# An adaLN transformer block on one core: the first pairs' modulation split over two PSUM banks by engine, and w1's load gated by the b2 row

## The chip, the core and the metric

The kernel runs on one core of a Trainium2 chip. A core has TensorE (PE, matmuls; PEld is its weight loads), VectorE (DVE), ScalarE (ACT), GpSimd (POOL) and SyncE (SP, which issues most of the DMAs). Each engine works its own instruction list in order and waits for others through semaphores. The metric is the device time of one execution in microseconds. In a row of the order below, a name with `<-` is what an instruction writes and reads.

## What is computed

One transformer block on x of 2048 tokens by 448 features, with 16 heads of 28 and a hidden size of 1792:

```python
mod = (_silu(c) @ w_mod).reshape(c.shape[0], 6, 1, -1)      # sa, ca, ga, sb, cb, gb
h = _layernorm(x) * (1 + ca) + sa
x = x + ga * attention(h, A_wqkv, A_wo)    # each query sees 8 keys, 2 tokens apart, behind it
h = _layernorm(x) * (1 + cb) + sb
x = x + gb * (gelu(_layernorm(h) @ w1 + b1) @ w2 + b2)
```

## The kernel before

The tokens are split into 1024 rows by two halves s (even and odd tokens), so that a window with stride 2 becomes a dense window of 8 rows within a half. Eight "pairs" j of 128 rows hold both halves. Features are cut into 14 blocks of 64, two to a partition range, so a pair's transposed activations hT have 7 blocks kb of 128 partitions (the lower 64 hold one half's features, the upper the other's).

The function `build_plan` lists 669 operations with the tiles that they read and write. It also holds cost estimates for a planner that ran beforehand; they issue nothing. The planner's result is written in the file: the table ORDER names each operation and its engine (96A is operation 96 on ScalarE, D is VectorE, P TensorE, G GpSimd, S SyncE, X a DMA's landing), and SLOTS gives the buffer of each tile. The kernel issues the operations in that order, so each engine's instruction list follows from ORDER alone. A layer under it adds the semaphore waits. It lets no two engines work on one PSUM tile at a time, not even where both only read.

The front, up to about 21 us, goes like this:

- SyncE loads x, the modulation weights (w_mod) and the raw query and key weights. The raw weights land in a staging tile, which shares its memory with w1 and is printed as `w`.
- "wpad" operations (L249 on ScalarE, L251 on VectorE and GpSimd) copy these weights into a padded layout, 28 columns into 32. There are 20 of them: for each kb, the part with m=0 serves the first half of the projection and the part with m=4 the second. They wait for three landings of the staging tile.
- VectorE and ScalarE take the layer norm's statistics (L365 to L370) and normalise the first two pairs (L386, L390) into zb.
- TensorE computes the modulation columns (L338, L341), which VectorE turns into the per-partition constants sa_c and ca_c (L352, L353). Then it transposes the two pairs' zb blocks (L430) into two PSUM tiles: blocks 0 to 3 into one and 4 to 6 into the other.
- The "hmod" operations (L401 on ScalarE, L403 on VectorE) read these tiles, apply the constants and write hT. For the first two pairs there are seven, one for each kb. ORDER gives kb 1, 2 and 6 to VectorE and 0, 3, 4 and 5 to ScalarE.
- One filler matmul (L304) stands ahead of the first query and key projection (L475). The projection's first part runs kb by kb, each step needing hmod kb and kb+1 and the m=0 copies of kb. Its results are evicted to qT and kT by L493 on VectorE and L491 on ScalarE; then come the first values (L516).

Further on, the pairs 2 and 3 are transposed on TensorE too (their hmods are two operations, of four and three blocks), and pairs 4 to 7 by DMA (L445). SyncE's queue then broadcasts the later modulation rows (L726 to L728, among them ga, which scales wo at L730), and loads wo, b1, b2, w1 and w2. These bulk loads are held back by gates: a one-element DMA (L175, written to the tile `gate`) reads the end of an earlier load and so makes SyncE wait for its landing. In `load`, an argument `at` registers a load as the next gate, and a load with `bulk` waits for the last one registered:

```python
if bulk and gate:
    after.append(gate[-1][0])
...
if at:
    gate.append((d, at))
```

w1's first load (L205) waits in this way for the last half of wo (L210). GpSimd combines the b2 row (printed `b_bc`) with a modulation row at L729. After attention come the output projection (L627, evicted at L630), the second layer norms, their DMA transposes (L656), and the two MLP matmuls (L676 with w1, L700 with w2).

Of the kernel before, what the change touches and what calls it, by code (L numbers as in the profile page):

```python
# [14 lines left out]
KB = 7  # L15
# [16 lines left out]
 'fill3': 1,  # L32
# [10 lines left out]
24S 81P 90D 91A 15X 94D 17X 93D 26S 51D 52G 55A 66D 95P 49A 53D 28S 59D 19X 57A 47D 92P 82D 65A 30S 64G 61D 63A 54D 60G 155P 97D 21X 96A 48G 98D 99A  # L43
32S 104D 58G 156P 100A 157P 62G 102D 23X 101A 158P 56D 80G 118D 106A 159P 25X 160P 50G 103D 161P 162P 134D 27X 29X 167P 105A 31X 163D 133D 165P 168A
# [113 lines left out]
def build_plan(cfg):  # L158
# [27 lines left out]
    def transpose(fn, rd, wr, uses):  # L186

        a = op("dti", {"SP": 1.24}, fn, rd=rd, wr=wr, uses=uses, lat=0.0)
        d = op("ld", {"DMA": 0.25}, None, wr=wr, uses=uses, after=[a], lat=1.7)
        a.land = d  # L190

    def c0(t):
        return PL + t
# [3 lines left out]
    def load_w(nm, dst, src, cuts, rate, bulk=False):  # L197
# [9 lines left out]
        for u in range(2):  # L207
# [3 lines left out]
            load("SP", 128 * n, f, [(nm, KB - 1 + 0.5 * u, KB - 0.5 + 0.5 * u)] + alias, issue=0.5, rate=rate / 2, bulk=bulk and u == 0, at=(lambda g: dst(g)[64:65, KB - 1, 0:1]) if bulk and u else None)  # L211
# [193 lines left out]
    for j in range(NP):  # L405
# [13 lines left out]
        if grp:  # L419
# [15 lines left out]
            if j == js[-1]:  # L435
                for kbs in [range(kb, kb + 1) for kb in range(KB)] if js[0] == 0 else (range(0, 4), range(4, KB)):
                    half = kbs[0] // 4

                    def f_hv(g, a=128 * js[0], w=w, kbs=kbs, ptr=ptr[half], e=None):
                        for kb in kbs:  # L440
                            modulate(g, e, kb, g.hT[:, kb, c0(a):c0(a + w)], g.psb(ptr.slot)[:, 0, kb % 4 * w:(kb % 4 + 1) * w])
                    op("hmod", {"ACT": 0.1 + 0.48 * len(kbs), "DVE": 0.08 + 0.325 * len(kbs)}, f_hv, rd=["sca"], wr=[(f"hTm{kb}", 128 * js[0], 128 * js[0] + w) for kb in kbs], uses=[ptr[half]], after=trs)
# [472 lines left out]
```

## Time and profile before

| what | value |
|---|---|
| runs | 182.71, 179.97, 179.34 us; median 179.97 |
| profiled execution | 179.01 us, of which the span from first to last instruction is 177.3 |
| granted TensorE clock, mean over the span | 0.99 of full speed |
| idle between 9 and 30 us: L475 for ScalarE's L401 | 1.5 us |
| idle: L401 for VectorE's L403, and the reverse | 1.5 us and 1.0 us |
| first L475 matmul; all 112 of the first projection | starts at 13.20 us; take 7.96 us |
| w1's gate (L175); w1's first issue | 40.23 us; 40.92 us |
| first MLP matmul (L676) | 73.44 us |

A row of a timeline gives start, length in us, engine, line, operation, what is written and read, and in brackets the idle time ahead of it with what ended it. A trailing x5 means five instructions in a row. A `q` behind an engine's name (SPq) is its queue issuing a DMA. A row of waits gives who waited for whom, the total in us, how often, and the longest.

### The profile page before, as it was taken

The numbers are of one execution on the slowest core, as the hardware profiler recorded it, in microseconds if no ns is written. First come the engines' busy times: TensorE is split into PE (matmuls) and PEld (weight loads), VectorE is DVE, ScalarE is ACT, GpSimd is POOL, SyncE is SP. The second block draws the span as 40 slices with busy tenths as digits, with TensorE's granted clock in tenths as the row PEclk, the third lists the DMA queues.
The fourth block names the chain that finished last, engine by engine and source line by source line (L and its number), as shares of the span: only waits on it lengthen the run. The fifth ranks groups of instructions, "written<-read, shape, count | busy, mean of one in ns | idle before, by whom it ended". The sixth has DMA issues, their size and how long they took to land.

```text
span 177.3 us, 7209 instructions
## 1 busy us (share of the span) xinstructions
PE 163.9 (92%) x3238; PEld 112.4 (63%) x3238; DVE 122.8 (69%) x251; ACT 104.0 (59%) x152; POOL 66.5 (37%) x96
## 2 busy tenths in 40 slices
PE   7959997978799969999999999999999999999991
PEld 2449866764454436789756679855589755885550
DVE  2778995984879999889496979983898982000231
ACT  5377889468176656678961168992258730893000
POOL 7562377022164641342921516240236560400300
PEclk9996999999999999999999999999999999999999
DMA  4999526656345324532032200006300042100102
GB/s 130 352 386 343 220 79 98 156 149 182 109 188 207 102 47 120 133 107 78 6 55 55 85 22 4 4 0 77 75 17 0 4 103 52 55 0 4 52 26 78
DMA packets 20472, 17.55 MB, mean 99 GB/s; under 512 B 11862, under 2 KB 18906, under 8 KB 20442
## 3 DMA queue, kind: packets, MB, share of 16 engines
q1 hardware_dynamic: 20428, 17.10, 34.0%
q8 instruction: 25, 0.41, 1.0%
q14 instruction: 5, 0.04, 0.1%
q10 hardware_dynamic: 14, 0.00, 0.0%
HBM read 12.51 MB, written 1.84 MB: 81 GB/s over the span
## 4 chain that ended last, share of the span: by engine, by line
PE 70%; DVE 8%; DMA 8%; SPq 5%; ACT 4%; issue 2%; DVEq 0%
PE ps L676 25%; PE ps L700 24%; PE ps L627 6%; PE ps L475 6%; PE ps L516 4%; DMA w<-in_A_wqkv_dram 4%; DMA w<-in_B_w_dram 3%; PE ps L580 2%; PE ps L551 2%; SPq L445 2%; DMA wo<-in_A_wo_dram 2%; ACT et L559 1%; DVE st L369 1%; DVE w L251 1%; DVE et L567 1%
## 5 line engine op out<-in xcount | busy, mean ns | idle before, releaser
L683 ACT ACTIVATE hmw<-ps,b1c 128x512 bf16<-128x512 f32 x56 | 37.9, 687 | 13.5 <-PE ps L676 10.0
L676 PE MATMUL ps<-yT,w 64*128 64x256 bf16 x784 | 44.4, 269 | 0.0
L700 PE MATMUL ps<-w,hmw 128*128 128x448 bf16 x224 | 43.8, 353 | 0.0
L676 PEld LDWEIGHTS <-w 64*128 64x128 bf16 x784 | 40.7, 94 | 3.1 <-issue 0.9
L700 PEld LDWEIGHTS <-hmw 128*128 128x128 bf16 x224 | 21.3, 98 | 19.6 <-issue 0.4
L475 PE MATMUL ps<-hT,w 64*128 64x256 bf16 (+1 forms) x336 | 27.4, 319 | 2.5 <-ACT hT L401 1.5
L691 POOL TENSOR_TENSOR x1p<-x_all,gbb 128x896 f32<-128x896 bf16 x8 | 15.1, 1894 | 38.4 <-DVE x_all L709 33.4
L475 PEld LDWEIGHTS <-w 64*128 64x128 bf16 x336 | 18.0, 99 | 10.1 <-issue 2.4
L709 DVE TENSOR_TENSOR x_all<-ps,x1p 128x896 bf16<-128x896 f32 x7 | 7.6, 1085 | 22.5 <-PE ps L700 22.5
L376 POOL TENSOR_TENSOR rs<-tv,neg_half 128x2 f32<-128x2 f32 (+1 forms) x20 | 15.7, 789 | 15.4 <-DVE tv L374 14.2
L369 DVE BATCH_NORM_STATS2 st<-x_all 128x6 f32<-128x448 bf16 x27 | 16.4, 609 | 2.6 <-DMA x_all<-in_A_x_dram 2.5
L559 ACT ACTIVATE et<-ps 128x912 bf16<-128x912 f32 x18 | 15.6, 930 | 2.7 <-PE ps L551 2.6
L627 PE MATMUL ps<-wo,hT 64*128 64x448 bf16 x112 | 11.8, 350 | 2.8 <-DMA w<-in_B_w_dram 1.4
L374 POOL TENSOR_SCALAR tv<-mv 128x2 f32<-128x2 f32 (+1 forms) x11 | 4.5, 411 | 24.1 <-DVE mv L370 13.4
L567 DVE TENSOR_TENSOR et<-et,mask 128x912 bf16<-128x912 bf16 x18 | 12.5, 711 | 1.5 <-ACT et L559 1.4
L516 PE MATMUL ps<-wv,hT 64*64 64x448 bf16 x252 | 12.9, 351 | 0.0
L683 ACT ACT_TABLE_LOAD x3 | 3.8, 1283 | 12.3 <-PE ps L676 6.7
L630 DVE TENSOR_TENSOR x_all<-ps,x_all 128x896 bf16<-128x896 f32 x8 | 8.7, 1085 | 2.6 <-PE ps L627 2.5
L627 PEld LDWEIGHTS <-hT 64*128 64x128 bf16 x112 | 5.3, 94 | 8.0 <-DVE hT L613 3.9
L593 DVE TENSOR_TENSOR on<-ps,rden 128x896 bf16<-128x896 f32 x9 | 9.8, 1085 | 0.2
L369 DVE BATCH_NORM_STATS2 st<-h 128x6 f32<-128x448 bf16 x16 | 9.7, 607 | 0.3 <-POOL h L644 0.2
L516 PEld LDWEIGHTS <-hT 64*64 64x64 bf16 x252 | 7.0, 107 | 4.4 <-issue 0.6
(100 smaller groups left out, 199.1 us busy)
## 6 DMA issues: line engine op xcount, KB each, us to landing
w<-in_B_w_dram SPq DMA_DIRECT2D x3, 896.0 KB, 4.7
out_dram<-x_all SPq DMA_DIRECT2D x7, 224.0 KB
x_all<-in_A_x_dram SPq DMA_DIRECT2D x3, 448.0 KB
hmw<-in_w_mod_dram SPq DMA_DIRECT2D x1, 1344.0 KB
w<-in_B_w_dram SPq DMA_DIRECT2D x2, 448.0 KB, 3.5
hmw<-in_w_mod_dram SPq DMA_DIRECT2D x1, 672.0 KB
wv<-in_A_wqkv_dram SPq DMA_DIRECT2D x2, 336.0 KB
wo<-in_A_wo_dram SPq DMA_DIRECT2D x2, 336.0 KB
```

Source lines behind the costliest of these rows:

```text
L369: g.nc.vector.bn_stats(out=g.stats[nm][:, i, :], in_=x)
L376: op(kind, {"POOL": 0.92}, lambda g: g.nc.gpsimd.tensor_tensor(out=g.rs[nm][:], in0=g.tv[nm][:], in1=g.neg_half[:, 0:n], op=ALU.pow), rd=[ ...
L475: g.nc.tensor.matmul(o[:, s, x:x + n], lhsT=g.wqk[r0:r0 + 64, kb, m, :], rhs=g.hT[r0:r0 + 64, k, c0(t0):c0(t0 + n)], start=(kb == 0 and (n ...
L516: g.nc.tensor.matmul(o[64 * half:64 * half + 64, s, 0:D], lhsT=g.hT[r0:r0 + 64, (kb + s) % KB, ka:ka + 64], rhs=g.wv[r0:r0 + 64, kb, :], s ...
L559: g.nc.scalar.activation(out=g.ebufs[et.slot][:, 912 * hf:912 * hf + 912].rearrange("p (r c) -> p r c", r=2), in_=g.ps[lt.slot][:, :, 0:8 ...
L567: (g.nc.vector if e == "DVE" else g.nc.gpsimd).tensor_tensor(out=v, in0=v, in1=g.mask[:].rearrange("p a b -> p (a b)"), op=ALU.mult)
L593: g.nc.vector.tensor_tensor(out=g.onb[rd_.slot][:].rearrange("p s (h d) -> p s h d", h=H), in0=o[:, :, :, 0:DH], in1=g.rden[rd_.slot][:].u ...
L627: g.nc.tensor.matmul(o[:, s, 0:D], lhsT=g.hT[r0:r0 + 64, (kb + s) % KB, c0(128 * j):c0(128 * j + 128)], rhs=g.wo[r0:r0 + 64, kb, :], start ...
L676: g.nc.tensor.matmul(o[:, s, 0:n], lhsT=g.w1[r0:r0 + 64, kb, ft * 128:(ft + 1) * 128], rhs=g.yTb[yT.slot][r0:r0 + 64, (kb + s) % KB, 0:n], ...
L683: g.nc.scalar.activation(out=g.hmv(hm.slot)[:, ft, :, 0:n], in_=g.ps[p1.slot][:, :, 0:n], func=ACTF.Gelu_apprx_tanh, bias=g.b1c[:, ft:ft + 1])
L691: op("x1p", {"POOL": 2.05}, lambda g, j=j, xp=xp: g.nc.gpsimd.tensor_tensor(out=g.x1pb[xp.slot][:], in0=g.x_all[:, j], in1=g.gbb2[:].unsqu ...
L700: g.nc.tensor.matmul(o[:, s, 0:D], lhsT=g.hmv(hm.slot)[:, ft, s, cc:cc + 128], rhs=g.w2[:, ft, :], start=(ft == 0), stop=(ft == FT - 1))
```

## The change

In the first pairs, the transposes of even kb now go to one PSUM tile and those of odd kb to the other. For the first group (pairs 0 and 1) the hmods of the first tile (kb 0, 2, 4, 6) may run on VectorE only and those of the second (1, 3, 5) on ScalarE only. The group of pairs 2 and 3 keeps two operations, now of the even and the odd blocks, both still on VectorE. ORDER's second and third line are replaced, which moves the wpad copies around the modulations; two fillers instead of one stand ahead of the projection. wo's last half is no longer registered as a gate; the b2 row is. The rest are planner's costs.

```diff
- 'fill3': 1,
+ 'fill3': 2,
...
-24S 81P 90D 91A 15X 94D 17X 93D 26S 51D 52G 55A 66D 95P 49A 53D 28S 59D 19X 57A 47D 92P 82D 65A 30S 64G 61D 63A 54D 60G 155P 97D 21X 96A 48G 98D 99A
+24S 81P 90D 91A 15X 94D 17X 93D 26S 52G 47D 49A 51D 53D 55A 57A 95P 28S 19X 92P 82D 30S 64G 60G 155P 96D 21X 98D 97A 100D 59D 99A 102D 61D 101A 48G
...
-        a = op("dti", {"SP": 1.24}, fn, rd=rd, wr=wr, uses=uses, lat=0.0)
-        d = op("ld", {"DMA": 0.25}, None, wr=wr, uses=uses, after=[a], lat=1.7)
+        a = op("dti", {"SP": 1.45}, fn, rd=rd, wr=wr, uses=uses, lat=0.0)
+        d = op("ld", {"DMA": 0.25}, None, wr=wr, uses=uses, after=[a], lat=2.1)
...
-            load(..., at=(lambda g: dst(g)[64:65, KB - 1, 0:1]) if bulk and u else None)
+            load(..., at=(lambda g: dst(g)[64:65, KB - 1, 0:1]) if bulk and u and nm != "wo" else None)
...
-    load_w("wo", lambda g: g.wo, lambda g: g.A_wo, (0, 3, 6), 335e3, True)
+    load_w("wo", lambda g: g.wo, lambda g: g.A_wo, (0, 3, 6), 200e3, True)
...
-    load("SP", 115e3, lambda g, e: e.dma_start(out=g.b2_bc[:], in_=g.B_b2.partition_broadcast(128)), ["b2"], issue=0.4)
+    load("SP", 115e3, lambda g, e: e.dma_start(out=g.b2_bc[:], in_=g.B_b2.partition_broadcast(128)), ["b2"], issue=0.4, at=lambda g: g.b2_bc[0:1, 0:1])
...
-                    g.nc.tensor.transpose(out=g.psb(ptr[kb // 4].slot)[:, 0, kb % 4 * w + x:kb % 4 * w + x + 128], in_=z[:, kb, :], identity=g.ident[:])
+                    g.nc.tensor.transpose(out=g.psb(ptr[kb % 2].slot)[:, 0, kb // 2 * w + x:kb // 2 * w + x + 128], in_=z[:, kb, :], identity=g.ident[:])
...
-                for kbs in [range(kb, kb + 1) for kb in range(KB)] if js[0] == 0 else (range(0, 4), range(4, KB)):
-                    half = kbs[0] // 4
+                for kbs in [range(kb, kb + 1) for kb in range(KB)] if js[0] == 0 else (range(0, KB, 2), range(1, KB, 2)):
+                    half = kbs[0] % 2
...
-                            modulate(g, e, kb, g.hT[:, kb, c0(a):c0(a + w)], g.psb(ptr.slot)[:, 0, kb % 4 * w:(kb % 4 + 1) * w])
-                    op("hmod", {"ACT": 0.1 + 0.48 * len(kbs), "DVE": 0.08 + 0.325 * len(kbs)}, f_hv, ...)
+                            modulate(g, e, kb, g.hT[:, kb, c0(a):c0(a + w)], g.psb(ptr.slot)[:, 0, kb // 2 * w:(kb // 2 + 1) * w])
+                    op("hmod", {e: t for e, t in (("ACT", 0.1 + 0.48 * len(kbs)), ("DVE", 0.08 + 0.325 * len(kbs))) if js[0] or e == ("DVE", "ACT")[half]}, f_hv, ...)
```

What this does to VectorE's list, from the first weight copy on, before the change. Here `w_72<-w_71` is a wpad copy, `ps_63` holds the modulation columns, `ps_64` and `ps_62` are the two tiles of the transposes, and `st<-x_all` is a statistic:

```order
L251 COPY w_72<-w_71 64x16x28 x2
L251 COPY w_72<-w_71 128x16x28 x3
...
L353 TENSOR_SCALAR ca_c<-ps_63 64x7
L251 COPY w_72<-w_71 128x16x28 x2
L403 TENSOR_SCALAR hT<-ps_64,ca_c,sa_c 128x256 x2
L369 BN_STATS st<-x_all 128x6
L370 BN_AGGR mv<-st 128x2
L403 TENSOR_SCALAR hT<-ps_62,ca_c,sa_c 128x256
L251 COPY w_72<-w_71 64x16x28
```

And the same place of VectorE's list after the change:

```order
L251 COPY w_72<-w_71 128x16x28
L251 COPY w_72<-w_71 64x16x28
L251 COPY w_72<-w_71 128x16x28
...
L353 TENSOR_SCALAR ca_c<-ps_63 64x7
L403 TENSOR_SCALAR hT<-ps_64,ca_c,sa_c 128x256 x3
L251 COPY w_72<-w_71 128x16x28
L403 TENSOR_SCALAR hT<-ps_64,ca_c,sa_c 128x256
L251 COPY w_72<-w_71 128x16x28
L251 COPY w_72<-w_71 64x16x28
L251 COPY w_72<-w_71 128x16x28
L369 BN_STATS st<-x_all 128x6
```

The modulations moved ahead of four of the copies and of the first statistic; there are four of them, all from `ps_64`, and the eight copies in front of the query eviction are still eight.

ScalarE's list at the same place, as the difference:

```order
-L249 COPY w_72<-w_71 64x16x28 x5
-L401 ACTIVATE hT<-ps_64,sa_c,ca_c 128x256 x2
-L401 ACTIVATE hT<-ps_62,sa_c,ca_c 128x256 x2
+L249 COPY w_72<-w_71 64x16x28 x3
+L401 ACTIVATE hT<-ps_62,sa_c,ca_c 128x256 x3
+L249 COPY w_72<-w_71 64x16x28 x2
```

Two of the five copies moved behind the modulations, of which there are now three, all from `ps_62`.

SyncE's queue at w1's gate, with the semaphores that each DMA waits for (each DMA counts on one of eight, DMAHW0 to DMAHW7):

```order
 L235 DMA b_bc<-in_B_b_dram 128x448
 L727 DMA ga<-mdr 128x448 [waits DMAHW1_49]
-L175 DMA gate<-wo 1x1 [waits DMAHW6_49,DMAHW4_49,DMAHW2_49]
+L175 DMA gate<-b_bc 1x1 [waits DMAHW4_49,DMAHW2_49,DMAHW0_49]
 L205 DMA w_71<-in_B_w_dram 128x2x1792 [waits DMAHW3_49]
```

The gate stays at its place in the queue, behind b2 and ga and ahead of w1; it now reads the b2 row, and waits for that row's landing (DMAHW0) where it waited for wo's (DMAHW6).

More of the change, by code (lines that the diff above doesn't have):

```diff
@@ L210, in f @@
                 e.dma_start(out=dst(g)[64 * u:64 * u + 64, KB - 1, :], in_=src(g)[r0:r0 + 64])
-            load("SP", 128 * n, f, [(nm, KB - 1 + 0.5 * u, KB - 0.5 + 0.5 * u)] + alias, issue=0.5, rate=rate / 2, bulk=bulk and u == 0, at=(lambda g: dst(g)[64:65, KB - 1, 0:1]) if bulk and u else None)
+            load("SP", 128 * n, f, [(nm, KB - 1 + 0.5 * u, KB - 0.5 + 0.5 * u)] + alias, issue=0.5, rate=rate / 2, bulk=bulk and u == 0, at=(lambda g: dst(g)[64:65, KB - 1, 0:1]) if bulk and u and nm != "wo" else None)
     def load_x(a, b, q="SP"):
```

6 lines of the change are left out of this document (3 added, 3 removed).

## The prediction

> **What bounds the kernel now.** I read the page's first part, the waits of the front, the timelines of VectorE and ScalarE up to the first query eviction, the busy time by clock stretch, and last the places where the front hands over to the rest.
>
> ```profile
> PE 163.9 (92%) x3238; PEld 112.4 (63%) x3238; DVE 122.8 (69%) x251; ACT 104.0 (59%) x152; POOL 66.5 (37%) x96
> ```
>
> TensorE is busy for 163.9 us, 92% of the span, and the change takes no matmul away, so only the other 8%, its waiting, and time in which its clock is low can be won. The waits between 9 and 30 us show what the change aims at:
>
> ```profile
> PE ps L475 <- ACT hT L401: 1.5, 1, 1.5
> ACT hT L401 <- DVE hT L403: 1.5, 3, 0.6
> DVE hT L403 <- ACT hT L401: 1.0, 2, 0.6
> ```
>
> The two engines that modulate the first transposes (L401 on ScalarE, L403 on VectorE) wait for each other in turn, 1.5 + 1.0 us, and TensorE's first projection waits 1.5 us for them. VectorE's rows until it evicts the first query tile (L493):
>
> ```profile
> 9.37 1.48 DVE L251 COPY w<-w 64x448 bf16<-64x448 bf16 x5 [0.61 <-DMA w<-in_A_wqkv_dram]
> 10.76 0.15 DVE L352 COPY sa_c<-ps 64x7 f32<-64x7 f32 x1
> ...
> 11.09 0.16 DVE L353 TENSOR_SCALAR ca_c<-ps 64x7 f32<-64x7 f32 x1
> 11.28 0.82 DVE L251 COPY w<-w 128x448 bf16<-128x448 bf16 x2
> 12.13 0.41 DVE L403 TENSOR_SCALAR hT<-ps,ca_c,sa_c 128x256 bf16<-128x256 bf16 x1
> 13.18 0.41 DVE L403 TENSOR_SCALAR hT<-ps,ca_c,sa_c 128x256 bf16<-128x256 bf16 x1 [0.63 <-ACT hT L401]
> 13.51 0.62 DVE L369 BATCH_NORM_STATS2 st<-x_all 128x6 f32<-128x448 bf16 x1
> 14.16 0.18 DVE L370 BATCH_NORM_AGGREGATE mv<-st 128x2 f32<-128x6 f32 x1
> 14.68 0.41 DVE L403 TENSOR_SCALAR hT<-ps,ca_c,sa_c 128x256 bf16<-128x256 bf16 x1 [0.34 <-ACT hT L401]
> 15.12 0.27 DVE L251 COPY w<-w 64x448 bf16<-64x448 bf16 x1
> ...
> 17.91 1.23 DVE L493 CAST qT<-ps 128x1024 bf16<-128x1024 f32 x1 [0.19 <-PE ps L475]
> ```
>
> The reader is to see that VectorE idles only 0.63 + 0.34 + 0.19 = 1.16 us between its first copy and L493. For the last 0.19 it waits for TensorE, so both reach 17.91 almost together: an earlier TensorE alone gives 0.19 us. After it VectorE has no room:
>
> ```profile
> 17.91:26.50 8.59, 8.44 (x198) 6.26 (x194) 8.45 (x19) 7.35 (x18) 4.60 (x7) 1.00 0.41 145
> ```
>
> The columns are length, busy PE, PEld, DVE, ACT and POOL, granted clock, DMA share and GB/s. VectorE is busy for 8.45 of 8.59 us. What it does there feeds everything: both query evictions, the normalisation constants, the key eviction. So I follow the front on VectorE.
>
> **TensorE and its clock.** The same view by stretches of 3.41 us, then the first projection:
>
> ```profile
> 10.13:13.54 3.41, 1.32 (x20) 0.92 (x18) 2.68 (x13) 2.42 (x5) 2.76 (x5) 1.00 1.08 388
> 13.54:16.96 3.42, 3.42 (x38) 3.00 (x34) 2.92 (x10) 2.79 (x7) 1.00 (x3) 0.50 1.07 326
> 16.96:20.37 3.41, 3.41 (x66) 3.41 (x64) 3.15 (x7) 2.66 (x8) 1.14 (x2) 1.00 0.91 357
> 27.20:30.61 3.41, 2.71 (x100) 2.37 (x101) 1.46 (x6) 3.41 (x6) 2.64 (x4) 1.00 0.65 102
> 13.20 7.96 PE L475 MATMUL ps<-hT,w 64*128 64x256 bf16 x112 [1.52 <-ACT hT L401]
> ```
>
> A stretch with 1.32 us of work was followed by one at clock 0.50, which passed 38 matmuls where the next passed 66. The missing 28, at 3.41/66 = 0.052 us, are 1.45 us lost. After the change the stretch 10.13 to 13.54 holds the transposes, two fillers and nearly 2 us of the projection, and I expect no drop.
>
> **The change, part by part.** (a) ScalarE now has its own PSUM bank.
>
> ```profile
> 9.37 2.65 ACT L249 COPY w<-w 64x448 bf16<-64x448 bf16 x5 [1.06 <-DMA w<-in_A_wqkv_dram]
> 15.13 0.56 ACT L401 ACTIVATE hT<-ps,sa_c,ca_c 128x256 bf16<-128x256 bf16 x1 [0.48 <-DVE hT L403]
> ```
>
> Three copies instead of five before the modulations, at 2.65/5 = 0.53, end at 10.97. Three modulations of at most 0.56 end by 12.65 and the two moved copies by 13.71, where before the last modulation ended at 15.69: some 2 us earlier. No row shows both engines modulating at once; the nearest has both evicting from PSUM:
>
> ```profile
> 19.66 1.01 ACT L491 CAST kT<-ps 128x1024 bf16<-128x1024 f32 x1 [0.66 <-PE ps L475]
> 19.81 1.19 DVE L493 CAST qT<-ps 128x1024 bf16<-128x1024 f32 x1
> ```
>
> They overlap, and the VectorE one is no longer than the 1.23 of 17.91, so I add nothing. [...]
>
> (b) TensorE's first projection starts with ScalarE's first modulation, at 10.97 + 0.56 = 11.53 instead of 13.20. With the clock kept it ends about 1.67 + 1.45 = 3.1 us earlier, near 18.0. The second filler stands before it, while TensorE waits for the modulations anyway; if that cover were gone it would cost TensorE an estimated 0.2 us, four times the 0.052 us of a projection matmul, which runs on half the columns and beside another. The bank that each transpose writes changes nothing in their number.
>
> (c) VectorE, which decides. Its rows give three copies at 1.48/5 = 0.30 until 10.26 and four constants of together 0.49 (10.76 to 11.25) until 10.75. Then come four modulations instead of three. They stand in one piece, with the shape they have in a later row:
>
> ```profile
> 26.93 1.36 DVE L403 TENSOR_SCALAR hT<-ps,ca_c,sa_c 128x256 bf16<-128x256 bf16 x4
> ```
>
> So they take 1.36 and end at 12.16. Four copies now lie among and behind them, and their price is the open one:
>
> ```profile
> L251 DVE COPY w<-w x8: 271/275/631, 9.4 to 15.1; 128x448 bf16<-128x448 bf16 x5, 64x448 bf16<-64x448 bf16 x3
> 11.47 0.63 DVE L251 COPY w<-w 128x448 bf16<-128x448 bf16 x1
> 10.60 3.15 POOL L251 COPY w<-w 64x448 bf16<-64x448 bf16 x5 [0.54 <-DMA w<-in_A_wqkv_dram]
> ```
>
> The median copy takes 0.275 us, and the longest, 0.63, is the one that started at 11.47, inside GpSimd's run of copies. That run goes without a break from 10.60 to 13.75, just where the four moved copies now stand. All four undisturbed cost 1.1 us, all four disturbed 2.5; I take the middle, 1.8, since a copy can also start in front of GpSimd's next one. The statistics (L369) then start at 12.16 + 1.80 = 13.96 instead of 13.51, 0.45 later. Of the 4.40 us from there to L493 the piece from 14.34 to 15.12 (the 0.34 wait and the modulation) goes, 0.78, and the 0.19 wait: 3.43 remain. L493 starts at 17.39 instead of 17.91: **-0.52 us**. With the copies at their ends it is -1.2 or +0.2.
>
> [...]
>
> (d) From L493 on everything behind is shifted by the same amount, because each link waits for the one before:
>
> ```profile
> 39.35 0.43 SPq L727 DMA_DIRECT2D ga<-mdr  x1
> 40.23 0.65 SPq L175 DMA_DIRECT2D gate<-wo  x1
> 42.71 2.17 DVE L730 TENSOR_TENSOR wo<-wo,ga 128x3136 bf16<-128x3136 bf16 x1 [1.59 <-DMA ga<-mdr]
> 42.19 1.03 POOL L729 TENSOR_TENSOR gbb<-mb,b_bc 128x448 f32<-128x448 bf16 x1 [4.26 <-DMA b_bc<-in_B_b_dram]
> 45.42 1.50 PE L627 MATMUL ps<-wo,hT 64*128 64x448 bf16 x14 [1.36 <-DMA w<-in_B_w_dram]
> 58.08 2.29 SPq L210 DMA_DIRECT2D w<-in_B_w_dram  x2
> 64.42 1.26 SPq L656 DMA_TRANSPOSE yT<-zb  x1
> 73.44 0.94 PE L676 MATMUL ps<-yT,w 64*128 64x256 bf16 x14
> ```
>
> SyncE's queue reaches the ga row at 39.35, VectorE waits 1.59 us for it at 42.71, and the output projection follows at 45.42. The landing that this row names comes within 0.1 us of VectorE's eviction that the matmul needs. I take the shift as whole.
>
> (e) w1's load now waits for the b2 row instead of wo's last half. GpSimd's wait for b2 ended by 42.19, the old gate passed at 40.23: w1 starts about 1.9 us later against the rest. Behind the gate in SyncE's queue stand only w1 and its gates, until the transpose at 64.42. w1's last issue ends at 58.08 + 2.29 = 60.37 and would end at 62.3, in front of 64.42; w1 is first used at 73.44. Cost 0; without these covers it would be 1.9 us. What ga gains from an emptier queue is between 0 and its whole wait, 1.59; as ga was issued 0.9 us ahead of w1's gate, I take 0.
>
> (f) The planner's costs (transposes 1.45 and 2.1, wo's rate) issue nothing. The second pair group keeps both its modulations on VectorE, four and three blocks: 0.
>
> Sum: -0.52. The profiled execution took 179.01 us, and the runs shown have the median 179.97, so 0.96 above it. I forecast 179.97 - 0.52 = **179.4 us**, and 178.5 in a run like the profiled one.
>
> **The rivals.** (1) The gain of TensorE goes through whole: 3.1 us, 176.9. It needs VectorE not to be the limit; 8.45 busy of 8.59 us speaks against it.
>
> (2) No gain: all four copies are disturbed, or the 0.5 us is lost on the way to 45.42. 180.0 to 180.2.
>
> (3) Slower: the low clock comes later instead. TensorE ends the projection 3.1 us earlier but its next inputs come only 0.5 us earlier, so 2.6 us of idleness move into the stretches from 18 to 31 us. At 39% busy (1.32 of 3.41) the clock fell, at 79% (2.71 of 3.41) it did not; if a stretch that now comes out between 50 and 60% falls, the next runs at half speed and loses up to 1.7 us: 181.1. It decides from the point where the bound lies above such a share. TensorE's 1.36 us of waiting at 45.42 could swallow most of it.
>
> [...]
>
> (4) The later w1 reaches the path: 179.4 + 1.9 = 181.3. It needs the 13 us between 60.37 and 73.44 to be used up, and I see nothing that does.
>
> **How the numbers follow.** The forecast 0.57, rival (1) 0.08, (2) 0.18, (3) 0.14, (4) 0.03. Two per cent, 3.6 us, is about what a measurement of this kernel can tell from no change. Under 176.4 only the upper part of (1) ends, with clock and waits both better than worked out: 0.06. Over 183.6 would be (3) in two stretches together with (4) or something unseen: 0.08. Within: 0.86. The range goes from the undisturbed copies in a run like the profiled one (179.01 - 1.2 = 177.8) to rival (3), 181.0; it leaves out (1), (4) and the far tails, less than 2 in 10.
>
> **What would show it.** Right: no waits between L401 and L403 in the front; L475's first matmul near 11.5 and clock 1.00 from 13.54 to 16.96; L493's first row 0 to 1.2 us earlier and not waiting for TensorE; VectorE copies of 0.6 us between 12 and 14; the second query eviction as what the first values' matmuls (L516) wait for. Wrong: L493 earlier by 2 us or more; a new stretch at clock 0.50; a later w1 landing ahead of L676's first wait.

## The result, and the profile after

| | before | after |
|---|---|---|
| median of 21 runs each, us | 179.49 | 179.54 |
| ratio, 95% interval | 1 | 1.0004 (0.9979 to 1.003) |
| profiled execution: time, span, mean granted clock | 179.01, 177.3, 0.99 | 179.77, 178.1, 0.979 |
| first copy to first L493 on VectorE, us | 17.91 - 9.37 = 8.54 | 17.45 - 9.59 = 7.86 |
| first copy on VectorE to first L627 on TensorE, us | 45.42 - 9.37 = 36.05 | 46.29 - 9.59 = 36.70 |
| first L627 to the end of the span, us | 177.3 - 45.42 = 131.9 | 178.1 - 46.29 = 131.8 |

The time did not change. Some executions are slower as a whole (one of the changed kernel took 183.0 us): the ratios, and the means of runs further on, leave them out, the medians do not, and of the profiles of e4 and e7, which are such executions, only the first 20 us of e7 are used. The weights land at other times from one execution to the next (VectorE's first copy starts between 9.10 and 10.08 us in the profiles used here), so the table counts from that copy. The front became 0.68 us shorter. By the first output projection the whole of it and 0.65 us more were gone, and behind that point the two profiles keep the same distance. So what took the gain back lies between 17 and 46 us.

TensorE's row of the page after the change; it was busy for 163.9 us before:

```profile
PE 165.4 (93%) x3239; PEld 112.6 (63%) x3239; DVE 123.3 (69%) x252; ACT 104.1 (58%) x151; POOL 66.3 (37%) x96
```

It works 1.5 us longer on the same matmuls and one filler, so its work has become slower, and not only its waiting longer.

VectorE's front after the change, to be held against the rows in the prediction:

```profile
9.59 1.11 DVE L251 COPY w<-w 128x448 bf16<-128x448 bf16 x3 [0.89 <-DMA w<-in_A_wqkv_dram]
...
11.21 1.05 DVE L403 TENSOR_SCALAR hT<-ps,ca_c,sa_c 128x256 bf16<-128x256 bf16 x3
12.17 0.47 DVE L251 COPY w<-w 128x448 bf16<-128x448 bf16 x1
12.56 0.40 DVE L403 TENSOR_SCALAR hT<-ps,ca_c,sa_c 128x256 bf16<-128x256 bf16 x1
12.88 1.29 DVE L251 COPY w<-w 128x448 bf16<-128x448 bf16 x3
14.08 0.62 DVE L369 BATCH_NORM_STATS2 st<-x_all 128x6 f32<-128x448 bf16 x1
...
17.45 1.19 DVE L493 CAST qT<-ps 128x1024 bf16<-128x1024 f32 x1
```

No row here has a bracket between the first copy and L493: VectorE does not wait at all any more. The price for it is in the four copies, 0.47 + 1.29 = 1.76 us. ScalarE's modulations, which run at the same time as VectorE's, take 1.48 us for three:

```profile
11.23 1.48 ACT L401 ACTIVATE hT<-ps,sa_c,ca_c 128x256 bf16<-128x256 bf16 x3
```

TensorE's first projection (L475), its second one, and the output projection:

```profile
11.68 6.49 PE L475 MATMUL ps<-hT,w 64*128 64x256 bf16 x112
...
20.56 1.52 PE L516 MATMUL ps<-wv,hT 64*64 64x448 bf16 x28 [0.75 <-DVE qT L493]
...
27.86 0.64 PE L551 MATMUL ps<-qT,kT 28*64 28x57 bf16 x32 [1.15 <-DVE hT L403]
28.43 7.49 PE L475 MATMUL ps<-hT,w 64*128 64x256 bf16 x84
...
46.29 1.50 PE L627 MATMUL ps<-wo,hT 64*128 64x448 bf16 x14 [0.96 <-DVE hT L613]
```

The first projection starts without a wait and takes 6.49 us instead of 7.96. Then TensorE waits for VectorE again and again, here for 0.75 and 1.15 us. And the second projection takes 7.49 us for its 84 matmuls. The busy time by clock stretch says why (columns as in the prediction):

```profile
10.16:13.58 3.42, 3.21 (x49) 2.59 (x48) 3.25 (x13) 3.32 (x7) 2.69 (x6) 1.00 1.05 385
13.58:16.99 3.41, 3.41 (x65) 3.07 (x62) 3.25 (x10) 3.23 (x10) 1.01 (x3) 1.00 1.09 318
...
20.40:23.81 3.41, 2.46 (x42) 1.66 (x41) 3.34 (x9) 2.78 (x6) 2.21 (x3) 1.00 0.12 45
23.81:27.23 3.42, 2.17 (x112) 1.44 (x113) 3.39 (x12) 2.94 (x7) 2.23 (x4) 1.00 0.38 105
27.23:30.64 3.41, 2.78 (x54) 2.08 (x55) 1.33 (x5) 2.63 (x4) 2.53 (x4) 0.50 0.79 109
30.64:34.06 3.42, 3.42 (x36) 2.40 (x34) 2.89 (x6) 1.01 (x1) 0.03 (x1) 0.50 0.60 128
```

The low stretch at 13.5 us is gone. Two low stretches stand at 27.23 to 34.06 instead, behind one in which TensorE was busy for 2.17 of 3.42 us (64%). VectorE, up to 27 us, is as full as before. The last piece is the ga row, which is issued 0.9 us later than before (40.25 against 39.35), and w1's gate:

```profile
40.25 0.68 SPq L727 DMA_DIRECT2D ga<-mdr  x1
43.01 0.64 SPq L175 DMA_DIRECT2D gate<-b_bc  x1
...
43.92 1.83 DVE L730 TENSOR_TENSOR wo<-wo,ga 128x3136 bf16<-128x3136 bf16 x1 [1.71 <-DMA ga<-mdr]
```

Between the second projection and ga stands the third projection (28 matmuls of L475). Here it is before the change, then after it:

```profile
38.60 1.71 PE L475 MATMUL ps<-hT,w 64*128 64x256 bf16 x28 [0.95 <-ACT vb L525]
```

```profile
39.86 1.71 PE L475 MATMUL ps<-hT,w 64*128 64x256 bf16 x28
```

Counted from the first copy it comes 1.04 us later after the change (30.27 against 29.23).

So there were three theories to tell apart. **Carried, and taken back by the clock:** the shift of VectorE's front reaches the end in full, but TensorE's idleness, now later, costs it the clock where it is on the path. **The transfers decide:** SyncE's queue and the landings between 30 and 46 us, those of the DMA transposes (L445) among them, set the time, and the front has slack. **The gate:** w1's later load eats the gain.

### The profile page after: what moved, and what is told of

It is laid out like the page before. It is cut to its first block, busy times and chain, and to the rows that moved or that the text cites. A ratio compares the mean times of both kernels' runs of the same rounds, so it can differ in the third digit from the quotient of the medians.

```text
span 178.1 us, 7211 instructions
## 1 busy us (share of the span) xinstructions
PE 165.4 (93%) x3239; PEld 112.6 (63%) x3239; DVE 123.3 (69%) x252; ACT 104.1 (58%) x151; POOL 66.3 (37%) x96
## 4 chain that ended last, share of the span: by engine, by line
PE 69%; DVE 13%; DMA 9%; SPq 3%; issue 3%; ACT 1%; DVEq 0%
PE ps L676 24%; PE ps L700 24%; PE ps L627 6%; PE ps L475 5%; DMA w<-in_A_wqkv_dram 4%; PE ps L516 3%; DMA wo<-in_A_wo_dram 3%; DVE st L369 2%; PE ps L580 2%; PE ps L551 2%; DMA ga<-mdr 2%; DVE hT L403 2%; DVE w L251 2%; DVE qT L493 1%; PE ps L603 1%
## 5 line engine op out<-in xcount | busy, mean ns | idle before, releaser
L683 ACT ACTIVATE hmw<-ps,b1c 128x512 bf16<-128x512 f32 x56 | 38.0, 688 | 13.5 <-PE ps L676 10.0
L676 PE MATMUL ps<-yT,w 64*128 64x256 bf16 x784 | 44.4, 269 | 0.0
L676 PEld LDWEIGHTS <-w 64*128 64x128 bf16 x784 | 40.7, 94 | 3.1 <-issue 0.9
L475 PE MATMUL ps<-hT,w 64*128 64x256 bf16 (+1 forms) x336 | 28.6, 328 | 0.1
L475 PEld LDWEIGHTS <-w 64*128 64x128 bf16 x336 | 17.8, 102 | 8.6 <-POOL w L251 0.4
L627 PE MATMUL ps<-wo,hT 64*128 64x448 bf16 x112 | 11.8, 350 | 2.4 <-DVE hT L613 2.3
L516 PE MATMUL ps<-wv,hT 64*64 64x448 bf16 x252 | 13.1, 351 | 0.9 <-DVE qT L493 0.7
L516 PEld LDWEIGHTS <-hT 64*64 64x64 bf16 x252 | 7.4, 107 | 5.2 <-issue 1.7
L627 PEld LDWEIGHTS <-hT 64*128 64x128 bf16 x112 | 5.3, 94 | 7.6 <-DVE hT L613 3.5
```

Source lines behind the costliest of these rows:

```text
L475: g.nc.tensor.matmul(o[:, s, x:x + n], lhsT=g.wqk[r0:r0 + 64, kb, m, :], rhs=g.hT[r0:r0 + 64, k, c0(t0):c0(t0 + n)], start=(kb == 0 and (n ...
L516: g.nc.tensor.matmul(o[64 * half:64 * half + 64, s, 0:D], lhsT=g.hT[r0:r0 + 64, (kb + s) % KB, ka:ka + 64], rhs=g.wv[r0:r0 + 64, kb, :], s ...
L627: g.nc.tensor.matmul(o[:, s, 0:D], lhsT=g.hT[r0:r0 + 64, (kb + s) % KB, c0(128 * j):c0(128 * j + 128)], rhs=g.wo[r0:r0 + 64, kb, :], start ...
L676: g.nc.tensor.matmul(o[:, s, 0:n], lhsT=g.w1[r0:r0 + 64, kb, ft * 128:(ft + 1) * 128], rhs=g.yTb[yT.slot][r0:r0 + 64, (kb + s) % KB, 0:n], ...
L683: g.nc.scalar.activation(out=g.hmv(hm.slot)[:, ft, :, 0:n], in_=g.ps[p1.slot][:, :, 0:n], func=ACTF.Gelu_apprx_tanh, bias=g.b1c[:, ft:ft + 1])
```

## The experiments

All times of experiments are medians with a ratio to runs of the kernel before on the same chip. "Low clock" is where a stretch at 0.50 lay in the profiled execution.

| kernel | median, us | ratio (95%) | first copy to L493 | low clock, us | first copy to L627 |
|---|---|---|---|---|---|
| before | 179.49 | 1 | 8.54 | 13.54 to 16.96 | 36.05 |
| after | 179.54 | 1.0004 (0.9979 to 1.003) | 7.86 | 27.23 to 34.06 | 36.70 |
| e1 after, old gate | 179.27 | 0.998 (0.9942 to 1.0018) | 7.86 | 28.33 to 31.75 | 36.56 |
| e2 before, new gate | 179.43 | 0.9998 (0.9959 to 1.0037) | 8.55 | 13.80 to 17.21 | 35.62 |
| e3 after, late fillers | 181.48 | 1.0123 (1.006 to 1.0185) | 7.86 | 39.99 to 43.41 | 37.88 |
| e4 after, ga early | 179.5 | 1.0007 (0.9975 to 1.004) | | | |
| e5 before, front fillers | 179.72 | 1.0001 (0.997 to 1.0032) | 8.28 | 27.62 to 34.44 | 37.26 |
| e6 after, late front | 180.32 | 1.0053 (1.0023 to 1.0084) | 9.19 | 28.92 to 32.34 | 37.18 |
| e7 after, copies to ScalarE | 177.87 | 0.9905 (0.9868 to 0.9942) | 6.93 | | |
| e8 after, old gate, rows early | 179.45 | 0.9987 (0.9959 to 1.0016) | 7.84 | none | 34.66 |
| e9 e7 with e8 | 178.22 | 0.9936 (0.991 to 0.9963) | 6.97 | 26.27 to 33.10 | 35.57 |
| e10 before, copies to ScalarE | 179.23 | 0.9998 (0.9965 to 1.0031) | 8.01 | 12.65 to 16.06 | 36.02 |
| e11 after, copies to GpSimd | 177.99 | 0.994 (0.9912 to 0.9968) | 6.95 | none | 33.97 |
| e12 e9, wo behind the transposes | 178.8 | 0.9934 (0.9897 to 0.9971) | 6.94 | 27.00 to 33.83 | 35.55 |

### e1 and e2: the gate, taken out and alone

```diff
 e1: the changed kernel
-    ... at=(...) if bulk and u and nm != "wo" else None)
+    ... at=(...) if bulk and u else None)
-    load("SP", 115e3, ... ["b2"], issue=0.4, at=lambda g: g.b2_bc[0:1, 0:1])
+    load("SP", 115e3, ... ["b2"], issue=0.4)
 e2: the kernel before, with the same lines the other way round
```

> The changed kernel with the old gate: w1's load waits for wo's last half again, all else as changed. Theory 'the gate is harmless' (nothing of w1 is needed before 73 us): w1's first issue goes back from 43.69 to about 41 us, the first MLP matmul keeps its place against the output projection (L627 to L676 stays at about 28 us), and the time stays within 0.4 us of the changed kernel, 179.1 to 179.9. Rival 'the later w1 eats the gain': 0.5 to 1.9 us faster than the changed kernel, 177.6 to 179.0.

> The kernel before with only the new gate (w1 behind the b2 row), the front untouched. Theory 'the gate is harmless': the ratio to before is 1.000 with at most 0.002 either way, w1's first issue moves from 40.92 to between 42 and 43.7 us, L627 stays at 45.4 if what it waits for is VectorE and not w1's landing, which the row of before names. Rival 'the later w1 costs': 0.5 to 1.9 us slower, 180.0 to 181.4; then L627 would still wait for w1's landing and move with it to about 47.

Neither moved the time by as much as its interval can show. The gate does what it says; here is w1's first issue without it on the changed front (e1), then with it on the old one (e2):

```profile
40.92 0.39 SPq L205 DMA_DIRECT2D w<-in_B_w_dram  x1
```

```profile
42.57 0.40 SPq L205 DMA_DIRECT2D w<-in_B_w_dram  x1
```

From the first L627 to the first L676, the matmul that needs w1, it is 28.0 us before, 27.9 after, 27.9 in e1 and 27.9 in e2. L627 stayed at 45.22 in e2, though w1 landed later, so w1's landing, which the row of before names as its releaser, is not what it needs. By the rows the gate is out as a cause. By the times alone a cost of 0.7 us (the upper end of e2's interval, 1.0037) can't be excluded.

### e5: the clock kept in the old front

Seven fillers instead of one, in time in which TensorE waits.

```diff
 the kernel before
- 'fill3': 1,
+ 'fill3': 7,
```

> The kernel before with seven fillers instead of one ahead of the first projection, in TensorE's idle time from 11.3 to 13.0 us: it takes the low clock from the first projection and leaves the banks, the order and the gate alone. Theory 'VectorE decides the front': clock 1.00 from 13.5 to 17, the 112 matmuls of the projection take about 6.5 us instead of 7.96, but the first L493 comes only 0.1 to 0.2 us earlier (17.7 to 17.8 instead of 17.91), the second L493 stays at 19.8, and the time is 179.3 to 179.6. Rival 'TensorE's lost 1.45 us is on the path': 178.0. Third, 'the low clock comes later instead': a stretch at 0.50 between 20 and 45 us, time 179.5 to 181.

First VectorE's first eviction, then TensorE's two projections, in e5:

```profile
17.70 1.19 DVE L493 CAST qT<-ps 128x1024 bf16<-128x1024 f32 x1
```

```profile
13.25 2.11 PE L475 MATMUL ps<-hT,w 64*128 64x256 bf16 x33 [0.21 <-ACT hT L401]
15.80 4.52 PE L475 MATMUL ps<-hT,w 64*128 64x256 bf16 x79 [0.43 <-ACT hT L401]
28.66 7.56 PE L475 MATMUL ps<-hT,w 64*128 64x256 bf16 x84
```

The clock stayed in the front. The 112 matmuls took 6.63 us instead of 7.96, TensorE ended them 0.89 us earlier behind the first copy (20.32 - 9.42 = 10.90 against 21.16 - 9.37 = 11.79), and VectorE's L493 came 0.26 earlier (8.28 against 8.54). The time is the same, but the third case came too: in the profile of e5 the clock fell at 27.62 for two stretches, where before it had not. So the equal time alone does not show that TensorE's time in the front is worth nothing. Only two of e5's 12 runs kept a full clock; they took 177.75 and 178.07 us, about 1.2 us under the 179.12 of the kernel before on that chip and near the 178.0 of the rival. Two runs settle nothing, so that point stays open. The stretch in front of the drop was 64% busy:

```profile
24.21:27.62 3.41, 2.19 (x112) 1.44 (x113) 3.38 (x12) 3.35 (x8) 2.22 (x4) 1.00 0.05 14
27.62:31.03 3.41, 2.94 (x56) 2.21 (x57) 0.85 (x4) 2.71 (x4) 2.04 (x4) 0.50 1.04 134
```

This is the low clock's move alone, without banks, order or gate: take the wait and the low clock out of the front, and the low clock stands some 14 us later.

### e3: the clock kept between 23 and 34 us

22 more fillers in TensorE's later idle time; nobody reads their results. The edit is shown in short.

```diff
 the changed kernel, in f_tr, in later_mod and in f_lt
+                [matmul(ptr[1] bank 1, ident, 512 columns) for k in range(2) if j == 3]
+            [matmul(mb bank 1, ident, 512 columns) for k in range(2)]
+                [matmul(o[:, k % 2, 456:512], ident, 56 columns) for k in range(18) if n < 2 and lt.slot == 3]
```

> The changed kernel with 22 more filler matmuls (2 behind the transposes of pair 3, 2 behind the modulation rows L721, 18 short ones behind the third L551 group), in TensorE's idle time from 23.5 to 27.9 us; their results are read by nobody. Theory 'late clock' (the gain of the front was given back because TensorE ran at 0.50 from 27.23 to 34.06): no stretch at 0.50 before 35 us, the 84 matmuls of the second projection take about 4.8 us instead of 7.49, first L580 at about 33.4 instead of 35.85, L627 at about 45.0 instead of 46.29, time about 178.3. Rival 'SyncE's chain' (the gain was given back in SyncE's queue, whatever the clock): the clock is kept too, but ga is still issued near 40 us, VectorE's L730 still waits over 1 us for it, L627 at 45.7 or later, and the time stays at 179.2 to 179.6.

This is a miss in both theories' numbers: slower by 1.2%. The clock was kept to 39.99, the second projection took 4.76 us, and L580 came at 33.38, all as the clock's theory said. But the next thing that TensorE needs is hT from the DMA transposes. ScalarE's rows for it, in the changed kernel and in e3:

```profile
38.20 0.81 ACT L401 ACTIVATE hT<-hT,sa_c,ca_c 128x512 bf16<-128x512 bf16 x1 [2.76 <-DMA hT<-zb]
```

```profile
38.23 0.81 ACT L401 ACTIVATE hT<-hT,sa_c,ca_c 128x512 bf16<-128x512 bf16 x1 [5.77 <-DMA hT<-zb]
```

The landing is the same, whether TensorE is early or not. So TensorE only waited longer, and lost the clock there:

```profile
36.58:39.99 3.41, 1.00 (x70) 0.90 (x64) 1.75 (x5) 1.76 (x3) 0.90 (x1) 1.00 0.40 106
39.99:43.41 3.42, 3.42 (x57) 2.65 (x54) 1.11 (x3) 1.73 (x3) 1.03 (x1) 0.50 0.33 74
```

```profile
39.88 3.10 PE L475 MATMUL ps<-hT,w 64*128 64x256 bf16 x28 [1.49 <-ACT vb L525]
```

The third projection started at 39.88, as in the changed kernel (39.86), and took 3.10 instead of 1.71 us. That is 1.39 us, and L627 came 1.13 later. It explains the profiled execution. The one run of e3 with a full clock took 180.12, so more than the clock makes it slow, and what that is stays open.

The equal start, 39.88 and 39.86, also speaks against the clock's theory: as far as two executions can be compared, the low clock had cost the changed kernel nothing up to there that the transposes would not have cost it anyway. The projection's releaser, L525, stands in ScalarE's list right behind the L401 that waits for them. In nine of the twelve profiles used here the third projection starts 1.65 to 1.66 us behind ScalarE's first row on the transposed hT, the row shown above; only in e5, e9 and e12, each with two low stretches ahead of it, is TensorE itself the later one. And that landing did not follow the front. The last of the four transposes was issued 24.48 us behind the first copy before the change and 23.56 after, but ScalarE's row started at 27.57 and 28.62. Between 26 and 40 us the queue moved nearly as many packets (4462 and 4518), but they took 58.0% of the DMA engines' time before and 78.6% after. Why they took longer, no run shows.

### e6: the front made later on purpose

```diff
 the changed kernel
-                g.nc.vector.bn_stats(out=g.stats[nm][:, i, :], in_=x)
+                [g.nc.vector.bn_stats(out=g.stats[nm][:, i, :], in_=x) for _ in range(3 if nm == "a2" and i == 1 else 1)]
```

> The changed kernel with one statistic of VectorE (L369, the first one, ahead of the first L493) issued three times over, with the same result: two more of 0.57 us, so that the first L493 comes at about 18.6 instead of 17.45, later than in the kernel before (17.91). Theory 'the shift of the front is carried whole' (the prediction's step): L627 and the end 1.15 us later, 180.7. Theory 'the transfers from 30 to 46 us decide' (SyncE's queue and the landings of wo, the transposes and the rows): the front has slack, L627 moves by 0.6 us or less, time 179.5 to 180.1.

```profile
9.10 1.11 DVE L251 COPY w<-w 128x448 bf16<-128x448 bf16 x3 [0.41 <-DMA w<-in_A_wqkv_dram]
...
18.29 1.19 DVE L493 CAST qT<-ps 128x1024 bf16<-128x1024 f32 x1
```

L493 came 9.19 us behind the first copy, 1.33 later than in the changed kernel, and the time rose by 0.0053 - 0.0004 = 0.5%, 0.9 us (by the interval of e6 0.3 to 1.4). The expected 1.15 lies inside, but 0.6 does too. In the profile L627 came only 0.48 us later (37.18 against 36.70 behind the first copy), as the transfers' theory had it, in an execution with one low stretch where the changed kernel's had two. The next three kernels are the same question in the other direction.

### e7, e11 and e9: the front made shorter

Two of VectorE's copies (66 and 54 in ORDER) go to ScalarE, behind its own last two, or to GpSimd, behind its last.

```diff
 e7: the changed kernel, ORDER
-... 101A 48G 66D 54D 63A 65A 32S
+... 101A 48G 63A 65A 66A 54A 32S
 e11: the changed kernel, ORDER
-... 101A 48G 66D 54D 63A 65A 32S ... 160P 50G 103D
+... 101A 48G 63A 65A 32S ... 160P 50G 66G 54G 103D
```

> The changed kernel with two of VectorE's four copies that collide with GpSimd's (0.59 and 0.28 us, started at 13.29 and 13.89) moved to ScalarE, behind its own last two. Price of the copies as read from the changed kernel: the first statistic starts at about 13.3 instead of 14.08 and the first L493 at about 16.7 instead of 17.45; if the collision only moves to the copies that stay, half of that. Theory 'the shift is carried whole': time 178.8. Theory 'the transfers decide': time within 0.3 of the changed kernel, 179.2 to 179.8, with L627 at 45.4 or later.

> The changed kernel with the same two copies moved to GpSimd, behind its last one, instead of to ScalarE. GpSimd idles there until 17.5. Theory 'VectorE decides': L493 about 6.9 us behind the first landing again, ScalarE's L491 back at about 7.7 us behind it (8.6 with the copies on ScalarE), the first L516 about 1 us earlier than there, and 0.988 to 0.991 of before. [...]

VectorE's rows in e11, and then TensorE's:

```profile
9.84 1.11 DVE L251 COPY w<-w 128x448 bf16<-128x448 bf16 x3 [1.09 <-DMA w<-in_A_wqkv_dram]
...
16.79 1.19 DVE L493 CAST qT<-ps 128x1024 bf16<-128x1024 f32 x1
```

```profile
11.93 3.60 PE L475 MATMUL ps<-hT,w 64*128 64x256 bf16 x60
16.26 3.01 PE L475 MATMUL ps<-hT,w 64*128 64x256 bf16 x52 [0.72 <-POOL w L251]
...
27.57 4.76 PE L475 MATMUL ps<-hT,w 64*128 64x256 bf16 x84
...
43.81 1.50 PE L627 MATMUL ps<-wo,hT 64*128 64x448 bf16 x14 [0.68 <-DVE hT L613]
```

L493 stands 6.95 us behind the first copy, 0.91 earlier than in the changed kernel, and the time is 0.994 of before; with ScalarE taking the copies it is 6.93 and 0.9905. By the ratios that is 1.8 us under the changed kernel (177.87 us, where 178.8 was expected), more than the 0.93 us by which L493 moved. In e11 the theory's number (0.988 to 0.991) did not come. TensorE now waits 0.72 us for GpSimd's copies, while VectorE's last copy took 0.27 us, as in the changed kernel (0.28). The first L516 comes only 9.36 us behind the first copy, where one microsecond less than e7's 9.62 was expected. The times of e7 and e11 do not differ beyond their intervals. e9 puts e7 and the early rows of e8 (below) together:

```diff
 e9: e7's ORDER, the old gate, and e8's order of the rows
```

> The two copies on ScalarE and the early rows with the old gate, together. Theory 'the front is carried, VectorE decides it' (the copies alone gave 0.9905 of before): the same again, 177.4 to 178.0 or 0.988 to 0.992 of before, and L493 about 6.9 us after the first landing of the weights as with the copies alone. If the rows' gain (L627 at 44.35 in their own profile) adds to it whole, 176.5. Theory 'the transfers decide': the copies' 0.9905 was chance, and the ratio comes back to 0.997 to 1.000.

0.9936, a little over the expected 0.988 to 0.992: the copies' gain was not chance, and the early rows add nothing to it. Its profile has two low stretches as the changed kernel's has, and its L627 stands 1.13 us earlier (35.57 against 36.70).

Put in a row, the front of the changed kernel at 9.19, 7.86 and 6.95 us (e6, after, and e7, e9 and e11 together) stands at ratios of 1.0053, 1.0004 and 0.9905 to 0.994. Over 2.24 us of front that is between 1.1% and 1.5%, or 2.0 to 2.7 us. So a shift of VectorE's front is carried about in full over this row as a whole; the steps differ (0.9 us for 1.33 in e6, 1.2 to 1.8 for 0.9 in the others), and their intervals are wide. With this the theory that the front has slack has fallen as the rule. By the same row a front of 8.54 us would stand at about 1.003 to 1.005, and the kernel before stands at 1: it lacks some 0.5 to 0.9 us of loss that the changed kernel has.

### e10: the copies moved in the kernel before

```diff
 the kernel before, ORDER
-... 55A 66D 95P ... 61D 63A 54D 60G 155P ... 102D 23X 101A
+... 55A 95P ... 61D 63A 60G 155P ... 102D 23X 101A 66A 54A
```

> The kernel before with two of VectorE's copies (of the same two weight blocks) moved to ScalarE behind its last modulation; banks, fillers and gate as before. Theory 'the two PSUM tiles in common chain the engines': the modulations still wait for each other and TensorE still loses its clock, so the first L493 stays at 17.7 to 17.9 and the time at 0.998 to 1.001 of before; the copies are worth something only once the banks are split. Rival 'a VectorE copy is worth its length wherever it stands': 0.6 to 0.7 us less, 0.996, or as much as with the split, 0.991.

```profile
11.15 0.41 DVE L403 TENSOR_SCALAR hT<-ps,ca_c,sa_c 128x256 bf16<-128x256 bf16 x1
...
17.19 1.23 DVE L493 CAST qT<-ps 128x1024 bf16<-128x1024 f32 x1 [0.18 <-PE ps L475]
```

The time came as expected (0.9998), but L493 did not: it stands 8.01 us behind the first copy instead of 8.54. One of the two copies had stood ahead of the first modulation, which now starts 0.8 us earlier behind the first copy. The interval reaches down to 0.9965, so a gain of 0.53 us (0.997) is not excluded. What is shown is that the same move without the split gives less than with it, since e7's interval ends at 0.9942.

### e4, e8 and e12: the transfers

e4 moves the ga row (L727) ahead of L728. e8 does that with the old gate, and issues the b1 and b2 rows ahead of wo's first part. e12 is e9 with wo's second part behind the second two transposes.

```diff
 e4, ORDER (e8 makes the same move, and issues the two rows right behind 34S)
-... 128X 215S ... 45X 214S 148D
+... 128X 214S 215S ... 45X 148D
 e8, build_plan, with the old gate
+    load("SP", 3500, ... ["b1r"], issue=0.4)
+    load("SP", 115e3, ... ["b2"], issue=0.4)
     load_w("wo", ...)
-    load("SP", 3500, ... ["b1r"], issue=0.4)
-    load("SP", 115e3, ... ["b2"], issue=0.4, at=...)
 e12, ORDER of SyncE
-mdr, gate, wo second part, two transposes, ga
+mdr, two transposes, gate, wo second part, ga
```

> The changed kernel with the ga broadcast (L727) moved ahead of the other rows (L728) in SyncE's queue, some 5.5 us earlier; nothing else. Theory 'SyncE's chain': ga is issued at about 34.6 us and lands before 39, VectorE's L730 (43.92 in the changed kernel, after 1.71 us of waiting for ga) starts without that wait at about 42.2, L627 at about 44.6 instead of 46.29, time 178.0 to 178.6. Theory 'late clock': L627 is held by TensorE's own lateness, stays near 46 where the low clock comes, and the time stays at 179.2 to 179.6. A third possibility: wo's last halves, now 0.4 to 0.7 us later in the queue, hold L730 instead of ga; then half or less of the 1.71 is won, 179.0.

> The changed kernel with the old gate, the b1 and b2 rows issued ahead of wo's first part (SyncE's queue is idle there from 13.6 to 23.0 us), and the ga row ahead of the other rows (L728): 1.6 to 2 us of SyncE's issues and three transfers leave the stage from 34 to 41 us. Theory 'the transfers decide': ga lands by 39, TensorE's L737 and VectorE's L730 no longer wait for a row, L627 at 44.4 to 45.0 instead of 46.29 (45.66 without the b2 gate), time 178.0 to 178.5. Rival 'TensorE's and VectorE's own work fill the stage': L627 stays at 45.5 or later, 179.2 to 179.6. Third: the transposes' landing (38.1 in the changed kernel) holds everything whatever the rows do; then ScalarE's first L401 on hT stays at 38.2 and the gain is under 0.4.

> The combination of copies and rows, and wo's second part (336 KB, with its gate) issued behind the second two transposes instead of ahead of them. Theory 'the transposes' landing holds TensorE at 36 to 40 us': they leave about 1 us earlier and land at about 35 instead of 36.2 to 38.3, L475's third projection about 1 us earlier, time 0.5 to 0.8 us under the combination without it. Rival 'SyncE's order moves the wait to wo': wo's second part and last halves land 1 to 2 us later and VectorE's L730 waits for them; time the same within 0.3 us or up to 1 us slower.

None of the three gained beyond its interval: 1.0007, 0.9987, and e12 at 0.9934 against e9's 0.9936. The profile of e8 looks like a hit, though, with L627 at 44.35, just where the transfers' theory put it:

```profile
28.30 4.76 PE L475 MATMUL ps<-hT,w 64*128 64x256 bf16 x84
...
44.35 1.50 PE L627 MATMUL ps<-wo,hT 64*128 64x448 bf16 x14 [0.70 <-DVE hT L613]
```

But this is an execution in which the clock never fell. It took 177.67 us, and it was the fastest of the 12; the median is 179.45. A single profile would have misled here. In e12 the wait only moved, to wo as its rival said:

```profile
43.29 1.79 DVE L730 TENSOR_TENSOR wo<-wo,ga 128x3136 bf16<-128x3136 bf16 x1 [1.61 <-DMA gate<-wo]
```

### What the clock costs, over all runs

Each run lists its mean granted clock. One stretch of 3.41 us at half speed takes half of 3.41 / 178, or 1%, off it, so 1.00, 0.99 and 0.98 stand for none, one and two of them. Of 86 runs of the kernel before, beside the experiments, 73 have one, and their mean is 179.28 us; the three with none have 179.27, and the ten with two 179.94. By these three runs the stretch at 13.5 us costs nothing that can be seen. In the changed kernel the three runs at 0.997 or more have a mean of 178.74 us and the other 16 have 179.56. The same two means are 178.22 and 179.27 in e1, 177.91 and 179.39 in e5, 177.67 and 179.25 in e8, 177.57 and 178.31 in e9, and 177.75 and 178.27 in e11 (2, 2, 1, 3 and 5 runs with a full clock). Single runs with a full clock were 0.0 us under the mean of the others in e6, 0.5 in e12, 1.0 in e10 and 1.7 in e7. In most kernels, then, the runs with a full clock are 0.5 to 1.6 us faster. This compares runs and changes nothing in them: where the stretch lay in a run without a profile is not known (in e10's own it lay in the front), and a run whose inputs come late may be slow and lose its clock for the same reason.

## Why the prediction was right, and where not

The time, 179.4 forecast and 179.54 measured, was right and inside the range, but by luck. Two errors in it cancel: the median of the three runs shown, 179.97, was high by 0.48 against the 21 runs, and the gain of 0.52 did not come.

- **(a) and (b), banks and TensorE: right.** L401 and L403 no longer wait for each other. Two engines modulating at once took 1.48 us for three on ScalarE and 1.05 for three on VectorE, within the 0.56 and 0.41 that the forecast had for one. The first matmul came at 11.68 (forecast 11.53), and the projection took 6.49 us at full clock.
- **(c), VectorE decides: right for L493, with its price.** The four copies were put at 1.8 us and took 1.76. L493 came 0.46 us earlier, or 0.68 counted from the first copy, against 0.52 forecast. (The sum's 12.16 is 0.05 more than its terms give, 10.75 + 1.36 = 12.11, and rival (3), worked out at 181.1, stands in the range as 181.0.) That an earlier TensorE moves L493 by little is shown by e5's 0.26 us; that it is worth nothing to the whole time is not shown.
- **(d), "I take the shift as whole": the step that failed.** It had everything behind L493 shifted by the same amount, "because each link waits for the one before". In the changed kernel's profile the 0.68 us won at L493 had become 1.04 us lost at the third projection and 0.65 us lost at L627. Two things stand there in place of the shift. One is rival (3), at 0.14: the low clock came later instead, here in two stretches, and in the profiles of e1, e3, e5, e6, e9 and e12 too. The other the prediction had not named: the third projection waits for the landing of the DMA transposes, which came later although they were issued earlier (the last one 0.92 us earlier behind the first copy, ScalarE's row on them 1.05 us later). e3 shows that without the first of the two the third projection would have come no sooner.
- **(e) and (f), gate and planner: right.** w1 started 2.8 us later than with the old gate (43.69 in the changed kernel, 40.92 in e1), or 2.3 counted from the first copy, where 1.9 was forecast, and L676 did not wait for it.

What is shown is that the low clock moves (behind 26 us in those seven profiles, which have no low stretch in the front, and at 12.7 to 13.8 us in before, e2 and e10, where the first projection still waits), and that other shifts of VectorE's front, in e6, e7, e9 and e11, do reach the time, about in full when taken together. What made up the zero stays open between the low clock and the landings. For the clock speaks an estimate that fits: 0.68 us won, and 0.82 us, in 16 runs of 19, lost. The two profiles whose clock never fell (e8, e11) also have the earliest L627, 34.66 and 33.97 us behind the first copy. Against it speaks the only kernel that took the late low clock out on purpose, e3, which kept full clock to 40 us, gained nothing there, lost it later, and was slower for a reason that is only partly known.

**A faster version**, by about 1% or less, came out of the experiments: the changed kernel with two more copies taken off VectorE, 0.9905 (0.9868 to 0.9942) of before with ScalarE taking them and 0.994 (0.9912 to 0.9968) with GpSimd.

## What to carry to other kernels

When an engine's wait is removed and its next input is not earlier, the wait only moves (here TensorE's 1.52 us ahead of the first projection went, and from 17.90 to 27.00 us it was busy for 6.41 us instead of 8.73); ask what it does where it lands. For TensorE that includes its clock (low from 13.54 us before the change and from 27.23 after it), so count its work in the stretches behind the change and not only in the one that is repaired. Look, too, for an input further on that does not come through the repaired chain, as the DMA transposes here. Once two engines no longer wait for each other, take work off the one that is full: the split alone gave nothing (1.0004), and the split with 0.9 us of copies moved gave 0.6 to 1%.

## What the runs showed of the hardware

The border of the clock. In the profiles the granted clock changes in steps of 3.41 us: it was low for 3.41 us in before and for 6.83 us in the changed kernel. TensorE's busy time in a stretch did not tell whether the next one was low: of the stretches at full clock in the twelve profiles used here, those followed by 0.50 have up to 2.25 us busy (e9), while 19 with 1.69 to 2.23 us were followed by full clock. One of these is in e1:

```profile
41.99:45.40 3.41, 1.69 (x14) 0.69 (x14) 2.15 (x2) 2.68 (x4) 1.03 (x1) 1.00 0.82 268
45.40:48.81 3.41, 3.15 (x90) 1.71 (x92) 2.87 (x6) 0.00 (x0) 0.35 (x1) 1.00 0.10 28
```

```profile
42.06 1.69 PE L475 MATMUL ps<-hT,w 64*128 64x512 bf16 x14
```

What tells them apart in the twelve profiles is the work: for each matmul the columns that it moves, times the rows and columns of the array that it uses. A row of the timeline has all three: 64*128 64x256 uses 64 rows and 128 columns of the array and moves 256. Taken as 1, that matmul is the unit here. e1's stretch holds the 14 matmuls of the last row, with 512 columns each, or 28 units. The changed kernel's stretch from 23.81 to 27.23, with more busy time, 2.17 us, holds these:

```profile
24.11 0.44 PE L551 MATMUL ps<-qT,kT 28*64 28x57 bf16 x32 [0.56 <-DVE kT L493]
24.48 0.94 PE L721 MATMUL ps<-hmw,silu_bc 128*32 128x448 bf16 x16
25.86 0.86 PE L551 MATMUL ps<-qT,kT 28*64 28x57 bf16 x64 [0.44 <-DVE hT L403]
```

An L551 is 0.049 units and an L721 0.875, so the stretch has 18.7, and the clock fell behind it. Summed in this way over the twelve profiles, a matmul across a border counted by its share, all 15 stretches at full clock that lost it have 21.8 units or less, and all 567 that kept it 24.6 or more; the fullest has 63. To come back took about as much: the four low stretches that stayed low have 21.6 to 23.6 units, and the ten that were followed by full clock 29.2 or more. So if it is one border, it lies near 24 units in these profiles, 38% of the fullest stretch. The 39% and 79% of busy time on which the prediction's rival (3) stood are not the measure: its stretch at 10.13 has 17.9 units. None of the ten stretches between 9 and 41 us that lost the clock was idle: TensorE was busy in them for 1.00 (e3) to 2.25 us (e9).

The grid of stretches was not tied to the kernel's start. The low clock of the front began at 13.54 us in the profile of before and at 13.80 in e2, but at 12.65 in e10, and a border of the changed kernel lay at 13.58. So the same work can fall into other stretches from one execution to the next, which fits that one and the same kernel has runs with none, one and two low stretches; a single profile does not show what a change does to the clock.
